# A spectral mixing and gated-convolution kernel: own buffers for the first stage of batch 0, a min form of the soft threshold, weight conversion in pairs of operations, operands at multiples of 128 bytes

## The chip, the core and the metric

The kernel runs on one core of a Trainium2 chip. The time is the device time of one execution in microseconds (us), the median of several; smaller is better. PE is the matrix engine (PEld its weight loads), DVE the vector engine, ACT the scalar engine, POOL the GpSimd engine, SP the engine whose queue issues all DMA transfers here. Each engine works through its own queue in order.

## What is computed

`x` is 8 x 3136 x 256. A real FFT along the sequence, a complex 256 x 256 mix with bias, a soft threshold, the inverse FFT; then a feed-forward layer with a convolution of three taps as its gate:

```python
X = np.fft.rfft(x, axis=1)
Yr = Xr @ w_r - Xi @ w_i + b_r
Yi = Xr @ w_i + Xi @ w_r + b_i
Yr = np.sign(Yr) * np.maximum(np.abs(Yr) - lam, 0.0)      # lam = 0.01, Yi likewise
x = np.fft.irfft(Yr + 1j * Yi, n=3136, axis=1)
h = np.maximum(x @ w_in, 0.0)                              # 256 -> 1024
conv_out = sum(conv_w[k] * shifted(h, k - 1) for k in range(3))
return h * sigmoid(conv_out) @ w_out                       # 1024 -> 256
```

`w_in`, `conv_w` and `w_out` arrive as float64 and are turned into two float32r parts, high and low, by integer operations on their bits.

## The kernel before

The length is split as 3136 = 56 x 56. The first half of the program is the spectral loop. For each batch, stage 1 (`stage1`, matmul L243) multiplies x by a 112 x 112 table, seven groups of four columns per batch; ACT copies each result from PSUM to `a1`, and a store writes `a1` to the DRAM scratch `sc1`. When all seven groups of a batch have landed, stage 2 reads them back transposed as `a2` (`load_a2`, L252). The loop goes over 56 items (8 batches x 7 groups). In iteration `it` stand: the load of `a2` for item it+2; stage 2 of item `it` (L262, 16 matmuls; ACT and DVE make `fh`, `fl`, `d` of it, L265 to L270); the mix of item it-1 (L286, 40 matmuls; ACT copies `p1`, DVE adds `v` in four parts, L294, then the threshold, L299 and L300; ACT rounds `v` to `sh`, L301, and POOL makes the rest `sl`, L302); stage 3 of item it-3 (L312, 12 matmuls, copied by ACT and stored to `sc2`); and stage 1 of later batches, some ten items ahead. Each matmul on float32 stands in the trace as two instructions, so an item's eight of L262 are 16 there and a stage 1 is four of L243.

The weights are loaded and converted inside this loop in eight pieces of 512 columns (`load_bits`, `from_bits`, `split_weight`, L194 to L211): every fifth iteration one piece is converted as a whole, by ten DVE operations and a copy on ACT. The convolution's weights (`load_conv`) follow in iteration 7.

The start differs: the seven groups of batch 0 go through the same buffers (three `xr`, two `a1`) with four PSUM buffers, the copies being shared by ACT and DVE (L245, L247). Tables and the weights of the mix are asked for after the last of these stores.

The second half, from about 600 us, is the feed-forward layer. Stage 4 (`stage4`, L389, seven per batch, each with one load of `z2` from `sc2`) ends the inverse transform: ACT writes `yh`, DVE `yl` (L395, L396). Then 28 chunks x 8 slices: `up` (L408, 12 matmuls of 450 columns), ReLU, the three taps, the sigmoid and the product on ACT and DVE, `gh` and `gl`; four slices later `down` (L436, 21 matmuls of 256 columns). The first batch's seven stage 4 have high priority.

A scheduler orders each engine's queue at compile time by a model of times, within the dependences; `tc.issue_after(ins)` puts what is traced in its block behind `ins` on that engine. Pools give out buffers (`bufs`) that are handed on when the last reader is done; with `reuse_waits="tile"` a new pool in old space waits for the tiles it overlaps alone. The lines on which the order around the change hangs:

```python
        DB, XRB, SL_ENG = 1, 3, nc.gpsimd
        AHEAD = NG + 3
        WP0, WPS = NG - 2, 5
```

## Time and profile before

| | |
|---|---|
| median of 3 runs | 1832.44 us (1827.99 to 1833.72) |
| profiled execution | 1831.85 us, its span 1830.0 us |
| busy in the span | PE 1778.5 (97%), PEld 1669.9 (91%), DVE 1557.2 (85%), ACT 1195.2 (65%), POOL 133.6 (7%) |
| DMA | 164.11 MB, mean 90 GB/s |
| granted TensorE clock | 0.989 of full speed |

Matmuls are pipelined: the profile lets each of them last until its results are out, so they overlap, and a busy PE is not a PE at its peak. A stage's rate is better read from the chain of waits, where consecutive pieces stand end to end, or from the count of instructions in a stretch. In rows of groups, after the bar, stand the busy time, the mean length of one in ns, and the idle time of the engine ahead of them with what ended it.

### The profile page before, as it was taken

The numbers are of one execution on the slowest core, as the hardware profiler recorded it, in microseconds if no ns is written. First come the engines' busy times: TensorE is split into PE (matmuls) and PEld (weight loads), VectorE is DVE, ScalarE is ACT, GpSimd is POOL, SyncE is SP. The second block draws the span as 40 slices with busy tenths as digits, with TensorE's granted clock in tenths as the row PEclk, the third lists the DMA queues.
The fourth block names the chain that finished last, engine by engine and source line by source line (L and its number), as shares of the span: only waits on it lengthen the run. The fifth ranks groups of instructions, "written<-read, shape, count | busy, mean of one in ns | idle before, by whom it ended". The sixth has DMA issues, their size and how long they took to land.

```text
span 1830.0 us, 29736 instructions
## 1 busy us (share of the span) xinstructions
PE 1778.5 (97%) x12320; PEld 1669.9 (91%) x12320; DVE 1557.2 (85%) x1788; ACT 1195.2 (65%) x1582; POOL 133.6 (7%) x60
## 2 busy tenths in 40 slices
PE   5889999999999899999999999999999999999998
PEld 3778789899899799999999999999999999999998
DVE  3899998888899598888888888888888888888887
ACT  2555556555555577777777667777767777776776
POOL 0122222222223100000000000000000000000000
PEclk8999999999999899999999999999999999999999
DMA  8676665665642311011111101111101111100001
GB/s 252 189 235 209 182 199 172 204 191 178 204 132 81 111 39 59 26 41 51 41 41 51 41 21 51 51 41 51 51 21 37 58 57 43 51 21 21 21 21 41
DMA packets 106682, 164.11 MB, mean 90 GB/s; under 512 B 8738, under 2 KB 85412, under 8 KB 106548
## 3 DMA queue, kind: packets, MB, share of 16 engines
q1 hardware_dynamic: 106548, 162.22, 29.4%
q8 instruction: 97, 1.59, 0.4%
q14 instruction: 37, 0.30, 0.1%
HBM read 85.13 MB, written 77.07 MB: 89 GB/s over the span
## 4 chain that ended last, share of the span: by engine, by line
PE 89%; DVE 6%; DMA 3%; issue 1%; ACT 0%; SPq 0%; ACTq 0%; DVEq 0%
PE acc L436 31%; PE ps_h L408 30%; PE ps_mx L286 12%; PE ps_s L389 5%; PE ps_s L262 4%; PE ps_s L243 3%; PE ps_s L312 3%; DVE v L294 1%; DVE fl L270 1%; DVE fl L268 1%; DMA a<-sc 1%; DMA sc<-a 1%; DVE v L300 1%; DMA z<-sc 1%; DMA t<-in_fwd_dram 0%
## 5 line engine op out<-in xcount | busy, mean ns | idle before, releaser
L436 PE MATMUL acc<-wout,gh 128*128 128x256 f32 x3136 | 578.3, 283 | 0.0
L417 DVE SCALAR_TENSOR_TENSOR c<-h,cw,c 128x896 f32<-128x896 f32 x448 | 513.0, 1147 | 52.7 <-ACT c L415 51.7
L408 PE MATMUL ps_h<-yh,win 128*128 128x450 f32 x1792 | 549.4, 367 | 1.3 <-ACT yh L395 1.2
L436 PEld LDWEIGHTS acc<-wout,gh 128*128 128x128 f32 x3136 | 497.0, 188 | 6.4
L436 PE MATMUL acc<-wout,gl 128*128 128x256 f32 x1568 | 441.0, 283 | 0.0
L410 ACT ACTIVATE h<-ps_h 128x900 f32<-128x900 f32 x224 | 207.6, 927 | 264.6 <-PE ps_h L408 264.4
L408 PEld LDWEIGHTS ps_h<-yh,win 128*128 128x128 f32 x1792 | 339.3, 189 | 27.3 <-ACT yh L395 1.5
L408 PE MATMUL ps_h<-yl,win 128*128 128x450 f32 x896 | 329.3, 368 | 0.4 <-DVE yl L396 0.4
L436 PEld LDWEIGHTS acc<-wout,gl 128*128 128x128 f32 x1568 | 294.1, 188 | 0.2
L423 DVE TENSOR_TENSOR gl<-c,gh 128x896 fp32r<-128x896 f32 x224 | 242.9, 1088 | 55.3 <-ACT gh L422 51.5
L419 DVE TENSOR_TENSOR c<-h,c 128x896 f32<-128x896 f32 x224 | 243.4, 1087 | 48.6 <-ACT c L418 48.1
L422 ACT CAST gh<-c 128x896 fp32r<-128x896 f32 x224 | 209.8, 942 | 49.2 <-DVE c L419 49.2
L418 ACT ACTIVATE c<-c 128x896 f32<-128x896 f32 x224 | 213.4, 953 | 26.1 <-DVE c L417 23.1
L286 PE MATMUL ps_mx<-wmix_lo,fh 128*128 128x256 f32 x672 | 202.4, 301 | 0.0
L286 PE MATMUL ps_mx<-wmix_hi,fl 128*128 128x256 f32 x672 | 193.4, 289 | 6.2 <-DVE fl L270 6.2
L286 PE MATMUL ps_mx<-wmix_hi,fh 128*128 128x256 f32 x672 | 197.5, 294 | 0.0
L408 PEld LDWEIGHTS ps_h<-yl,win 128*128 128x128 f32 x896 | 169.4, 189 | 10.3 <-DVE yl L396 0.9
L415 ACT ACTIVATE c<-h,cw 128x896 f32<-128x896 f32 x168 | 175.7, 1046 | 2.6 <-DVE gl L423 0.2
L302 POOL TENSOR_TENSOR sl<-v,sh 128x1024 fp32r<-128x1024 f32 x56 | 133.4, 2382 | 470.3 <-PE ps_s L312 289.0
L294 DVE TENSOR_TENSOR v<-ps_mx,p 64x512 f32<-64x512 f32 x224 | 153.9, 687 | 3.8 <-ACT p L288 0.3
L262 PEld LDWEIGHTS ps_s<-t,a 112*128 112x128 f32 x896 | 113.6, 199 | 42.5 <-DMA a<-sc 15.4
L286 PEld LDWEIGHTS ps_mx<-wmix_hi,fl 128*128 128x128 f32 x672 | 128.3, 191 | 16.6 <-issue 9.5
(90 smaller groups left out, 2145.8 us busy)
## 6 DMA issues: line engine op xcount, KB each, us to landing
xr<-in_x_dram SPq DMA_DIRECT2D x56, 448.0 KB, 4.5
sc<-a SPq DMA_DIRECT2D x56, 448.0 KB, 4.1
a<-sc SPq DMA_DIRECT2D x56, 448.0 KB, 4.8
sc<-z SPq DMA_DIRECT2D x56, 448.0 KB, 3.2
z<-sc SPq DMA_DIRECT2D x56, 448.0 KB, 3.8
out_dram<-o SPq DMA_DIRECT2D x27, 896.0 KB, 4.3
win_bits<-in_moe_w_in_dram SPq DMA_DIRECT2D x4, 512.0 KB, 4.9
wout_bits<-in_moe_w_out_dram SPq DMA_DIRECT2D x4, 512.0 KB, 5.2
```

Source lines behind the costliest of these rows:

```text
L262: nc.tensor.matmul(ps[:, k], a2[:, k, t * P:(t + 1) * P], t2[:, g * UG + k, :], start=(k == 0), stop=(k == UG - 1), skip_group_check=True)
L286: nc.tensor.matmul(ps[c][:, k, :], lt, rh, start=(n == 0), stop=(n == len(mm) - 1))
L294: nc.vector.tensor_tensor(v[dst, :, k, :], ps[c][src], p1[src], op=ALU.add)
L408: nc.tensor.matmul(ps[:, a, 0:CH + 2], lt, rh, start=(n == 0), stop=(n == len(mm) - 1))
L410: nc.scalar.activation(h, ps[:, :, 0:CH + 2], AF.Relu)
L415: nc.scalar.mul(c, h[:, :, 0:CH], cw[:, 0, f:f + 1])
L417: nc.vector.scalar_tensor_tensor(c, h[:, :, k:k + CH], cw[:, k, f:f + 1], c, op0=ALU.mult, op1=ALU.add)
L418: nc.scalar.activation(c, c, AF.Sigmoid)
L419: nc.vector.tensor_tensor(c, h[:, :, 1:CH + 1], c, op=ALU.mult)
L422: nc.scalar.copy(gh, c)
L423: nc.vector.tensor_tensor(gl, c, gh.bitcast(F32), op=ALU.subtract)
L436: nc.tensor.matmul(acc[m // 2][:, m % 2, :], lt[:, sl], rh[:, f, :], start=(f == 0 and n == 0 and m % 2 == 0), stop=(f == NF - 1 and n == ...
```

## The change

It has four parts.

- Head: the seven `x` loads of batch 0 go into seven buffers of their own (`hx`), the first one in two parts, and the results into seven buffers `ha`; the loads of tables, mix weights and bias stand between loads and stores. Two stages 1 of batch 1 are issued ahead of the first `a2` loads. The pools `wkf`, `wk`, `cab`, `io` are opened afterwards, in the space of these buffers.
- Threshold: instead of v - clip(v, -lam, lam) by two DVE operations, ACT makes r = relu(v - lam) and DVE one operation, min(v + lam, r).
- Weight conversion: `from_bits`, `split_weight` and `later` are generators now; from iteration 3 on two steps are taken per iteration, placed behind the threshold on DVE; from iteration 50 twelve. The convolution's weights come last.
- Places: `i2` and `cw` move behind the weights into one tile; rows of `y` get 3168 columns instead of 3138; small pads. In the program as built, all that PE reads in the second half, and `xr` and `f1`, starts at a multiple of 128 bytes. There are three `z2` buffers instead of two, and `h` has a pool of its own.

```diff
-    i2 = cst.tile([K1, K1], F32, name="i2")
-    cw = cst.tile([P, 3, NF], F32, name="cw")
+    cst.tile([P, 96], F32, name="pad")
     win = [cst.tile([P, NT, FF], F32R, name=f"win_{q}") for q in range(2)]
     wout = [cst.tile([P, NF, D], F32R, name=f"wout_{q}") for q in range(2)]
+    cst_s = cst.tile([P, 2 * P], F32, name="cst_s")
+    i2 = cst_s[0:K1, 0:K1]
...
-            v.tensor_scalar(e, hi, 20, 0x7FF, op0=ALU.logical_shift_right, op1=ALU.bitwise_and)
+            yield v.tensor_scalar(e, hi, 20, 0x7FF, op0=ALU.logical_shift_right, op1=ALU.bitwise_and)
...
+        def later():
+            pieces = []
...
+            for n in range(len(pieces) + 1):
+                if n < len(pieces):
+                    dst, src, nm = pieces[n]
+                    asked.append((dst, load_bits(src, WP, nm), WP, nm))
+                    yield None
+                if n:
+                    yield from split_weight(*asked.pop(0))
             nc.sync.dma_start(i2, inv2)
...
+        def stage1_head(xs, b=0):
+            with tc.tile_pool(name="ha", bufs=1, reuse_waits="tile") as ha:
+                for jc, xr in enumerate(xs):
+                    a1 = ha.tile([K1, JC, D], F32, name=f"ha{jc}")
...
-            cl = wk.tile([K2, UG, D], F32, name="cl", bufs=1)
-            nc.vector.tensor_scalar(cl, v, -LAM, LAM, op0=ALU.max, op1=ALU.min)
-            nc.vector.tensor_tensor(v, v, cl, op=ALU.subtract)
+            r = wk.tile([K2, UG, D], F32, name="r", bufs=1)
+            nc.scalar.activation(r, v, AF.Relu, bias=mlam)
+            thr = nc.vector.scalar_tensor_tensor(v, v, LAM, r, op0=ALU.add, op1=ALU.min)
...
-        WP0, WPS = NG - 2, 5
-        load_f1()
-        for p in range(NG):
-            ld = stage1(0, p, head=True)
-        with tc.issue_after(ld.ins):
-            load_t2(0)
-            load_mix()
-            load_bias()
+        WP0, LAST = 3, n_it - 6
+        load_f1()
+        with tc.tile_pool(name="hx", bufs=1, reuse_waits="tile") as hx:
+            xh = []
+            for p in range(NG):
+                xr, ld = load_x(hx, 0, p, parts=2 if p == 0 else 1, tag=f"hx{p}")
+                xh.append(xr)
+            with tc.issue_after(ld.ins):
+                load_t2(0)
+                load_mix()
+                load_bias()
+                st = stage1_head(xh)
+        with tc.issue_after(st.ins):
+            for _ in range(2):
+                stage1(*items[p1])
+                p1 += 1
+            for i in range(2):
+                a2s[i], ld = load_a2(*items[i])
...
-            while p1 < n_it and p1 < min(it + AHEAD, NG + 1 + it + it // 2):
+            while p1 < n_it and p1 < min(it + AHEAD, NG + 2 + it + it // 2):
...
-            if it == NG:
-                load_conv()
-            if it >= WP0 and it % WPS == 0 and later:
-                dst, src, nm = later.pop(0)
-                asked.append((dst, load_bits(src, WP, nm), WP, nm))
-            if it >= WP0 + WPS and it % WPS == 4 and asked:
-                split_weight(*asked.pop(0))
+            if WP0 <= it < n_it:
+                with tc.issue_after(ss[it - 1][2].ins):
+                    for _ in range(2 if it < LAST else 12):
+                        next(background, None)
...
-    zio, y_a = pool("zio", 2), pool("y_a")
-    wk, io, y_b = pool("cwk"), pool("cio"), pool("y_b")
+    zio, y_a = pool("zio", 3), pool("y_a")
+    wk, hp, io, y_b = pool("cwk"), pool("chp", 3), pool("cio"), pool("y_b")
+    SW = 3168
+    hp.tile([P, 8], F32, name="pad", bufs=1)
...
-        y = [(y_a, y_b)[b % 2].tile([P, NT, S + 2], F32R, name=nm) for nm in ("yh", "yl")]
+        y = [(y_a, y_b)[b % 2].tile([P, NT, SW], F32R, name=nm) for nm in ("yh", "yl")]
```

How the order of instructions moves is seen at three places. In the changed kernel line numbers differ: stage 1 of the head is L269 with copies L271 and L273, stage 1 L254, stage 2 L289, the mix L313, stage 3 L339, stage 4 L427, `up` L446, `down` L474.

SP's queue at the start, before: loads of `x` (L235) and stores of `a1` (L248) alternate from the fifth on, each load needing a free `xr`, each store its copies.

```order
L235 DMA xr_136<-in_x_dram 112x1024
L235 DMA xr_146<-in_x_dram 112x1024
L235 DMA xr_156<-in_x_dram 112x1024
L235 DMA xr_166<-in_x_dram 112x1024
L248 DMA sc1_0_57<-a1_138 112x1024
L235 DMA xr_176<-in_x_dram 112x1024
L248 DMA sc1_0_57<-a1_148 112x1024
L235 DMA xr_186<-in_x_dram 112x1024
L248 DMA sc1_0_57<-a1_158 112x1024
```

The same queue after, from the bias on; ahead of these rows stand the eight loads of `x` without a break, then t2 and the weights of the mix.

```order
L169 DMA b_raw_159<-in_b_i_dram 1x256
L274 DMA sc1_0_57<-ha0_167 112x1024
L274 DMA sc1_0_57<-ha1_175 112x1024
L274 DMA sc1_0_57<-ha2_183 112x1024
L274 DMA sc1_0_57<-ha3_191 112x1024
L274 DMA sc1_0_57<-ha4_199 112x1024
L274 DMA sc1_0_57<-ha5_207 112x1024
L274 DMA sc1_0_57<-ha6_215 112x1024
L245 DMA xr_225<-in_x_dram 112x1024
L245 DMA xr_235<-in_x_dram 112x1024
L279 DMA a2_245<-sc1_0_57 112x4x256
L279 DMA a2_247<-sc1_0_57 112x4x256
```

All loads of batch 0 now precede all stores, and two loads of batch 1 stand between the last store and the first `a2` load.

DVE's queue inside the loop where weights are converted, before: operations of a conversion (L194 to L211) stand between the four `v` of the mix (L294), between the two of the threshold (L299, L300), everywhere.

```order
L195 TENSOR_SCALAR win_e<-win_e 128x512
L270 TENSOR_TENSOR fl<-d,fh 128x2x256
L294 TENSOR_TENSOR v<-ps_mx_744,p_787 64x2x256 x2
L196 TENSOR_SCALAR win_e<-win_e 128x512
L294 TENSOR_TENSOR v<-ps_mx_745,p_787 64x2x256 x2
L197 SCALAR_TENSOR_TENSOR win_e<-win_bits,win_e 128x512
L299 TENSOR_SCALAR cl<-v 128x1024
L199 TENSOR_TENSOR win_m<-win_m,win_e 128x512
L202 SCALAR_TENSOR_TENSOR win_rest<-win_r,win_e 128x512
L300 TENSOR_TENSOR v<-v,cl 128x1024
```

DVE's queue after, one whole item from threshold (L327) to threshold.

```order
L327 SCALAR_TENSOR_TENSOR v<-v,r 128x1024
L194 TENSOR_SCALAR win_e<-win_e 128x512
L195 TENSOR_SCALAR win_e<-win_e 128x512
L294 TENSOR_TENSOR d<-ps_s_1413,d 128x256
L295 TENSOR_TENSOR fl<-ps_s_1413,fh 128x512
L294 TENSOR_TENSOR d<-ps_s_1422,d 128x256
L295 TENSOR_TENSOR fl<-ps_s_1422,fh 128x512
L321 TENSOR_TENSOR v<-ps_mx_1433,p_1476 64x2x256 x2
L297 TENSOR_TENSOR fl<-d,fh 128x2x256
L321 TENSOR_TENSOR v<-ps_mx_1434,p_1476 64x2x256 x2
L327 SCALAR_TENSOR_TENSOR v<-v,r 128x1024
```

Two operations of a conversion follow each threshold, and nothing stands between the last `v` and the threshold, which needs ACT's `r`.

SP's queue at the change to the second half, before: the first two loads of `z2` stand far ahead; the next ones follow the last stores of stage 3 (L315).

```order
L315 DMA sc2_7_72<-z1_6389 112x1024
L385 DMA z2_6491<-sc2_0_65 112x4x256
L385 DMA z2_6504<-sc2_0_65 112x4x256
L315 DMA sc2_7_72<-z1_6405 112x1024
L385 DMA z2_6517<-sc2_0_65 112x4x256
L385 DMA z2_6530<-sc2_0_65 112x4x256
L315 DMA sc2_7_72<-z1_6421 112x1024
```

The same place after.

```order
L423 DMA z2_6478<-sc2_0_65 112x4x256
L423 DMA z2_6491<-sc2_0_65 112x4x256
L423 DMA z2_6504<-sc2_0_65 112x4x256
L342 DMA sc2_7_72<-z1_6133 112x1024
L342 DMA sc2_7_72<-z1_6229 112x1024
L342 DMA sc2_7_72<-z1_6325 112x1024
L342 DMA sc2_7_72<-z1_6398 112x1024
L423 DMA z2_6517<-sc2_0_65 112x4x256
L423 DMA z2_6530<-sc2_0_65 112x4x256
L342 DMA sc2_7_72<-z1_6414 112x1024
```

Three loads now stand ahead of the last stores, and each later one stands one tile earlier against the stores.

More of the change, by code (lines that the diff above doesn't have):

```diff
@@ L237, in stage1 @@
             for j in range(0, JC, 2):
[L238 to L242 removed]
+                ps = ps1.tile([K1, 2, D], F32, name="ps_s1")
                 nc.tensor.matmul(ps, f1, xr[:, j:j + 2, :], start=True, stop=True)
[L244 to L247 removed]
+                nc.scalar.copy(a1[:, j:j + 2, :], ps)
@@ L248, in stage1 @@
             return nc.sync.dma_start(sc1[b][:, jc * JC:(jc + 1) * JC, :], a1)
+        def stage1_head(xs, b=0):
+            with tc.tile_pool(name="ha", bufs=1, reuse_waits="tile") as ha:
+                for jc, xr in enumerate(xs):
+                    a1 = ha.tile([K1, JC, D], F32, name=f"ha{jc}")
+                    for j in range(0, JC, 2):
+                        k = (jc * 2 + j // 2) % 4
+                        if k < 3:
+                            ps = psm.tile([K1, 2, D], F32, name="ps_s1h", tag=f"ps_mx{k}")
+                        else:
+                            ps = ps1.tile([K1, 2, D], F32, name="ps_s1")
+                        nc.tensor.matmul(ps, f1, xr[:, j:j + 2, :], start=True, stop=True)
+                        if j:
+                            nc.vector.tensor_copy(a1[:, j:j + 2, :], ps)
+                        else:
+                            nc.scalar.copy(a1[:, j:j + 2, :], ps)
+                    st = nc.sync.dma_start(sc1[b][:, jc * JC:(jc + 1) * JC, :], a1)
+            return st
@@ L315, in stage3 @@
             nc.sync.dma_start(sc2[b][:, g * UG:(g + 1) * UG, :], z1)
-        warm = stg.tile([P, 1], F32, name="warm")
+        nc.vector.memset(mlam, -LAM)
         nc.vector.memset(warm, 0.0)
```

94 lines of the change are left out of this document (45 added, 49 removed).

## The prediction

> **What bounds the kernel now.** I first read busy times by stage, cut where the page's TensorE row changes: the start, the early and the late spectral loop, its last items, the change to the second half, the second half. The columns are PE, PEld, DVE, ACT, POOL, clock, DMA share, GB/s.
>
> ```profile
> 0.00:42.00 42.00, 22.43 (x55) 11.35 (x56) 12.48 (x24) 10.64 (x19) 0.20 (x4) 0.81 0.83 249
> 42.00:254.00 212.00, 193.25 (x1343) 167.50 (x1341) 199.84 (x320) 115.68 (x204) 41.03 (x17) 0.97 0.69 202
> 254.00:519.00 265.00, 265.00 (x1966) 237.77 (x1964) 224.35 (x300) 155.04 (x274) 66.20 (x28) 1.00 0.63 187
> 519.00:596.00 77.00, 77.00 (x651) 76.50 (x650) 73.99 (x108) 43.70 (x74) 21.46 (x9) 1.00 0.36 106
> 596.00:639.00 43.00, 34.81 (x215) 32.09 (x215) 22.55 (x25) 21.31 (x22) 4.72 (x2) 0.88 0.41 118
> 639.00:1830.00 1191.00, 1185.96 (x8101) 1144.69 (x8100) 1024.01 (x1016) 848.80 (x991) 0.00 (x0) 1.00 0.13 40
> ```
>
> PE never stops from 254 to 596 nor, but for some 5 us at the end, from 639 on. Matmuls overlap, so what one costs comes from the chain, where nothing else stands between: item after item at 400 us, and the second half at 1016 us.
>
> ```profile
> 399.98 0.86 PE ps_s L243 x2
> 400.84 1.78 PE ps_s L262 x16
> 402.63 1.20 PE ps_mx L286 x10
> 403.83 0.86 PE ps_s L243 x2
> 404.69 3.60 PE ps_mx L286 x30
> 408.29 1.41 PE ps_s L312 x12
> ...
> 1015.96 1.68 PE ps_s L389 x15
> 1017.64 2.52 PE acc L436 x21
> 1020.16 2.46 PE ps_h L408 x12
> ```
>
> So 0.43 us for a matmul of L243, 0.111 for L262, 0.120 for L286, 0.1175 for L312, 0.112 for L389, 0.120 for L436, 0.205 for L408. An item of the spectral loop with its stage 1 takes 9.71 us, one without 7.99. The number of matmuls from 42 to 254 by line, L243, L262, L286, L312 in this order:
>
> ```profile
> 42.00:254.00 212.00, 43.99 (x83) 12.30 (x82) 0.97 0.69 202
> ...
> 42.00:254.00 212.00, 40.50 (x296) 38.51 (x295) 0.97 0.69 202
> ...
> 42.00:254.00 212.00, 113.25 (x760) 97.46 (x760) 0.97 0.69 202
> ...
> 42.00:254.00 212.00, 30.32 (x204) 25.96 (x204) 0.97 0.69 202
> ```
>
> At the prices above that is 35.7 + 32.9 + 91.2 + 24.0 = 183.8 us of work in 212: 28.2 us are lost there (18.75 of it idle, the rest half clock and pipeline refill behind the idle). In the same way 0 to 42 holds 30 matmuls of L243 and 26 of L262, 15.8 us, and loses 26.2; 596 to 639 holds 27 of L312, 128 of L389 and 60 of L408, 29.8 us, and loses 13.2. Nothing is lost between 254 and 596. All that the schedule can bring lies in these 67.6 us. Who held PE from 42 to 255, and at the change to the second half:
>
> ```profile
> PE ps_mx L286 <- DVE fl L270: 6.2, 4, 2.0
> PE ps_mx L286 <- DVE v L294: 4.9, 5, 1.6
> PE ps_s L262 <- DMA a<-sc: 3.5, 1, 3.5
> ...
> PE ps_s L389 <- DMA z<-sc: 6.5, 3, 3.5
> ```
>
> DVE is 94% busy from 42 to 254 (199.84 of 212), where the weights are converted.
>
> **The head.** The first item's first matmul is the row at 33.98; the chain of waits before it:
>
> ```profile
> 1.19 3.90 DMA xr<-in_x_dram
> 5.23 3.74 PE ps_s1h L243 x4
> 24.75 4.48 DMA sc<-a
> ...
> 29.31 0.34 SPq L252
> ...
> 30.23 7.09 DMA a<-sc
> ...
> 33.98 2.29 PE L262 MATMUL ps_s<-t,a 112*128 112x128 f32 x9 [10.89 <-DMA a<-sc]
> ...
> 12.00:15.00 3.00, 2.38 (x6) 0.62 (x4) 0.69 (x1) 0.59 (x1) 0.00 (x0) 1.00 0.99 336
> ```
>
> Before, a load waits for a buffer that a matmul frees, and stores wait behind such loads on SP's queue. Now seven loads go out at once, and the stores stand behind all of them and behind t2, the mix weights and the bias. What must have moved before the first a2 load is x (3.21 MB), the seven stores (3.21) and t2, f1 and the weights of the mix (0.8): 7.2 MB, at the 336 GB/s of the last row 21.5 us. The first 0.46 MB took until 5.1, so the stream began near 3.7 and ends at 25.2 if it never pauses. PE would be done earlier: from 4.4, four cold matmuls of 0.94 us (3.74/4) and 24 of 0.43 end at 18.5, copy and issue 1.0, a landing of 4.48 as in the row: 24.0. I take 24.5 for the last store. The pools that reuse the head's buffers write them after that and wait for nothing. Two x loads of batch 1 (0.92 MB, 2.7 us) are now queued ahead of the a2 loads; they move while SP waits for the last store, so a part of them hides. From SP's first issue of an a2 load, at 29.31, to the matmul it took 4.7 us. First item at 29.2 instead of 33.98; ends 26.5 and 32. Two halves of a new stage 1 (0.86) are done by then. The half clock that follows an idle PE stays: PE idles from 18.5 to 29 as it did from 24 to 34, and the rows of 0 to 42 and of 596 to 639 show 0.81 and 0.88 granted. Gain 5.6 with the moved stage 1, ends 3 and 8.
>
> **The threshold.** Removed on DVE, per item, are L299 and L300; added are one scalar_tensor_tensor there and one Relu on ACT:
>
> ```profile
> L299 DVE TENSOR_SCALAR cl<-v x56: 679/1576/2497, 58.6 to 597.3; 128x1024 f32<-128x1024 f32 x56
> ...
> L300 DVE TENSOR_TENSOR v<-v,cl 128x1024 f32<-128x1024 f32 x56 | 68.6, 1224 | 1.4
> L417 DVE SCALAR_TENSOR_TENSOR c<-h,cw,c 128x896 f32<-128x896 f32 x448 | 513.0, 1147 | 52.7 <-ACT c L415 51.7
> L301 ACT CAST sh<-v 128x1024 fp32r<-128x1024 f32 x56 | 58.8, 1050 | 82.1 <-DVE v L300 78.9 <-DVE cw L229 2.0 <-DVE cw_m L198 1.2
> L294 DVE TENSOR_TENSOR v<-ps_mx,p 64x512 f32<-64x512 f32 x224 | 153.9, 687 | 3.8 <-ACT p L288 0.3
> L210 DVE TENSOR_TENSOR win_m<-win_m,win 128x512 f32<-128x512 f32 x4 | 4.6, 1141 | 0.6 <-ACT win L209 0.6
> ```
>
> The new DVE operation is L417's kind on 1024 instead of 896: 1147 x 1024/896, at most 1.31, I take 1.28. DVE gives up 1.58 + 1.22 and takes 1.28: 1.5 us less per item. ACT takes 1.05 more; it was 155 of 265 us busy, so 5.7 of 9.71 becomes 6.8. In the late loop PE is the bound, and both are worth nothing there.
>
> The price is a new round trip: DVE waits for ACT between v (L294) and the threshold, and nothing of its queue stands between. Its loop per item is then four v 2.75, Relu 1.05, threshold 1.28, two conversions at most 2 x 0.69 (L210's undisturbed length, as L294's), d 2 x 0.42, fl 2 x 0.68, the last fl 0.69 (L267, L268 and L270 keep their shapes; 512 elements as in L294): 9.35. That is 0.36 below PE's 9.71. With 1.5 stages 1 per item, as early on, PE's item is longer still.
>
> **The weight conversion.** Ten DVE operations of each of eight pieces stood bunched in this stage, a piece every five items; now two operations follow each threshold from the fourth item on, at most 1.37 us per item, with the convolution's 27 small ones last. DVE's mean in the early loop falls from 94% to (8.2 - 1.5 + 1.4)/9.71 = 83%, 8.2 being the late loop's 224.35 over 27.3 items. The 11.1 us of waits for DVE in the list and the half clock behind them should go. What stays of 28.2: the wait for a2 at the change to batch 1 (3.5, and some 2.5 of half clock after it), since SP still holds that load until the last store of the batch has landed. I keep 6 and gain 22; ends 10 (all but the waits named DVE stay) and 27.
>
> From 519 to 596 no stage 1 is left and DVE was 96% busy against PE's 7.99 per item. There the round trip (10 items x 1.05) and the last 21 small operations, at
>
> ```profile
> L229 DVE TENSOR_TENSOR cw<-cw_m,cw_rest 128x8 f32<-128x8 f32 x3 | 0.5, 160 | 0.0
> ```
>
> 3.4 us, are set against 10 x 1.5 saved: near nothing. I take a loss of 1.5, ends 0 and 6.
>
> **The change to the second half.** Seven z loads feed its first tiles.
>
> ```profile
> 613.41 4.85 DMA z<-sc
> ...
> 620.76 1.12 ACT yh L395
> ...
> 621.90 1.13 DVE yl L396
> ```
>
> With two buffers the third to seventh were issued only when PE had read an earlier one, 4.85 us before they could be used; that is the 6.5 above. A third buffer moves each issue one tile earlier, some 2 to 3 us. But yh and yl, 2.25 us per tile, also hold the two PSUM buffers. Gain 3.5, ends 0 and 8.
>
> **Multiples of 128 bytes.** Before, i2 and cw (448 and 96 bytes) put win and wout 32 bytes past such a multiple, and a row of y of 12552 bytes puts its second half 8 further. After, all lie at a multiple. L286, whose operands lay so already, takes 0.120 for 256 columns; L436, off it, takes 0.120 as well: nothing to gain on 4704 matmuls. L408 has 450 columns. From the two, 0.44 ns per column; from L243 (two passes of 512 in 0.86, 0.42 each half) and L286's surplus 0.201 would be possible instead of 0.205: 2688 x 3.5 ns = 9.4 us at most, 0 at least. I take 3. The new places of h, z2, gh and gl change addresses alone, and PE covers what reads them.
>
> **Sum.** 5.6 + 22 - 1.5 + 3.5 + 3 = 32.6: span 1830.0 becomes 1797.4. The profiled execution took 1831.85 for its span, and the median of the runs, 1832.44, is 0.6 above it: 1800. With all ends at their best 1780, at their worst 1825.
>
> **Rivals.** (a) Slower: the round trip makes DVE the bound of the late loop. L299's median of 1576 against its shortest of 679 shows DVE held by POOL's subtraction (L302), and L210's mean of 1141 against 687 shows it for two SBUF operands. If the threshold and a conversion are each held 0.9, the loop is 11.15, 1.44 over PE's item; over 44 items that costs 63, and the time is 1863. It decides from 9.71 + 32.6/44 = 10.45 per item. Against it: Relu delays the threshold by just the time for which POOL held L299. Chance 4%.
>
> (b) Only the threshold is held, as L299 was, by 0.9: loop 10.25, 0.54 over, 44 items, 24 us: 1824. The Trainium skill says this, in SBUF — State Buffer, section SBUF: two separate sides: GpSimd and a DVE instruction with two SBUF inputs exclude each other for the whole instruction. By that rule the new operation, with v and r in SBUF, is no freer than the old one, and the sum is this 1824; without a meeting of the two it is 1800. The rows of L299 and L210 agree with the rule; whether the two meet depends on the time of Relu. Chance 10%.
>
> (c) The early loop is bound by DMA, not by DVE: the share of DMA is 0.83 in the first 42 us and i1, t2 and two weight pieces now queue up ahead of the fourth a2. Half of the 28.2 stays: 1808. For it: the share. Against: one wait of 3.5 named DMA. Chance 14%.
>
> (d) The alignment speeds all wide matmuls, L436 to L262's 0.111: 4704 x 9 ns and 9.4: 1752. Against it L286. Chance 5%.
>
> (e) Own buffers bring nothing in the head since DMA is the limit anyway: 1805, inside the forecast's range.
>
> **The numbers.** The forecast with (e) has 67%; a measurement of this kernel cannot tell less than 0.3%, 5.5 us, from no change. Faster by more: 0.67 + 0.14 + 0.05 and most of (b), 0.93 in all; within: 0.03; slower: 0.04. The range 1777 to 1821 takes in the forecast's ends but for the last 4 us, (c), and leaves out (a), (d) and most of (b).
>
> **What will show it.** The first matmul on a2 near 29; PE's idle time from 42 to 254 below 5 us, with DVE near 83%; the late item still 9.71; the seventh tile of the second half some 3 us earlier; L436 still 21 in 2.52, L408 12 in 2.42 to 2.46. I am wrong if waits for the threshold hold PE after 254, or if the matmuls of the second half change their pace by more than 2%.

## The result, and the profile after

The changed kernel takes 1806.47 us (median of 4 runs, 1805.84 to 1808.87) against 1833.08 for the kernel before on the same chip: a ratio of 0.9863, 95% interval 0.9842 to 0.9884. Its profiled execution has a span of 1807.1 us (before 1830.0) at a granted clock of 0.992.

The stretches answer to those of before, cut at the same events (columns as there):

```profile
0.00:42.00 42.00, 25.90 (x69) 12.31 (x70) 12.59 (x25) 11.48 (x22) 0.20 (x4) 0.80 0.93 263
42.00:254.00 212.00, 209.06 (x1529) 185.48 (x1529) 168.27 (x257) 146.53 (x249) 47.31 (x20) 1.00 0.70 214
254.00:519.00 265.00, 265.00 (x1993) 240.25 (x1993) 208.06 (x328) 182.85 (x306) 66.18 (x28) 1.00 0.62 188
519.00:574.00 55.00, 51.22 (x425) 50.10 (x423) 49.56 (x87) 33.27 (x51) 14.23 (x6) 1.00 0.33 98
574.00:615.00 41.00, 35.64 (x215) 33.18 (x214) 21.62 (x26) 23.04 (x25) 4.73 (x2) 0.88 0.42 124
615.00:1807.00 1192.00, 1187.56 (x8099) 1144.81 (x8098) 1023.79 (x1015) 848.04 (x990) 0.00 (x0) 1.00 0.13 40
```

The matmuls of 42 to 254 by line, L254, L289, L313, L339 in this order (PE, PEld, clock, DMA share, GB/s):

```profile
42.00:254.00 212.00, 47.09 (x92) 13.57 (x92) 1.00 0.70 214
...
42.00:254.00 212.00, 43.54 (x344) 41.96 (x344) 1.00 0.70 214
...
42.00:254.00 212.00, 123.86 (x865) 108.63 (x865) 1.00 0.70 214
...
42.00:254.00 212.00, 32.88 (x228) 28.48 (x228) 1.00 0.70 214
```

At the prediction's prices that is 39.6 + 38.2 + 103.8 + 26.8 = 208.3 us of work in 212: 3.7 lost, before 28.2. Counted in the same way, 0 to 42 holds 32 matmuls of stage 1, 25 of L289 and 12 of L313 (18.0 us; 24.0 lost, before 26.2); 519 to 574 holds 425 at 7.99/68 us (49.9; 5.1 lost, before none in the last items); 574 to 615 holds 24 of L339, 128 of L427, 60 of L446 and 3 of L474 (29.8; 11.2 lost, before 13.2). The second half takes 1192 for 8099 matmuls, before 1191 for 8101. So the 22.9 us between the two spans are +2.2 at the head, +24.5 in the early loop, -5.1 in the last items, +2.0 at the change to the second half and -1 behind it; that adds up to 22.6, and 0.3 is what counting at the cuts leaves.

The late item and the pace of the second half have not moved. From the chain of waits (the columns are start, length, what):

```profile
402.50 1.78 PE ps_s L289 x16
...
412.20 1.78 PE ps_s L289 x16
```

```profile
1016.18 2.46 PE ps_h L446 x12
1018.64 2.51 PE acc L474 x21
```

One item is 9.70 us, and 12 and 21 matmuls take what they took before to 0.01 us. The threshold (L327) in the late loop, shortest, median and longest in ns, and one of its operations with the POOL operation that it meets:

```profile
L327 DVE SCALAR_TENSOR_TENSOR v<-v,r x28: 1224/1369/1381, 258.3 to 516.8; 128x1024 f32<-128x1024 f32 x28
...
403.77 1.37 DVE L327 SCALAR_TENSOR_TENSOR v<-v,r 128x1024 f32<-128x1024 f32 x1 [2.11 <-ACT r L326]
...
401.70 2.36 POOL L329 TENSOR_TENSOR sl<-v,sh 128x1024 fp32r<-128x1024 f32 x1 [7.33 <-PE ps_s L339]
```

The head, however, came out otherwise than forecast. Its chain of waits, and with it two rows of the engines' own timelines (behind the bar of a timeline row, in brackets, stands the idle time ahead of it and what ended it):

```profile
19.41 0.64 DVE wm L158
...
24.69 4.81 DMA sc<-ha
...
29.65 5.09 DMA a<-sc
...
34.88 3.75 PE ps_s L289 x16
```

```profile
19.41 0.69 DVE L158 TENSOR_TENSOR wm<-wm_raw,wm_raw 128x512 f32<-128x512 f32 x1 [4.42 <-DMA wm_raw<-in_w_i_dram]
```

```profile
31.35 2.05 PE L254 MATMUL ps_s<-xr,f 112*112 112x512 f32 x2 [6.09 <-DMA xr<-in_x_dram]
```

The last store was issued at 24.69, where before it was issued at 24.75; the first stage 2 stands at 34.88, 0.9 later than before. DVE waited 4.42 us for the second half of the mix weights, with the copies of stage 1 queued behind, and PE 6.09 us for the first x of batch 1.

The 2.2 us that the head gained all the same did not come with the first item. The granted clock was 0.50 from 33 to 37 us in both kernels; in the changed one, where PE had stage 1 of batch 1 from 31.35 on, the full clock was back earlier. Before and after, from 40 to 45 us (PE, PEld, DVE, ACT, POOL, clock, DMA share, GB/s):

```profile
40.00:45.00 5.00, 5.00 (x27) 3.94 (x27) 2.08 (x5) 2.31 (x5) 0.00 (x0) 0.69 1.04 273
```

```profile
40.00:45.00 5.00, 4.97 (x37) 4.31 (x36) 3.88 (x8) 4.29 (x10) 0.00 (x0) 1.00 1.03 277
```

That the stage 1 brought the clock back is not shown by a run of its own.

### The profile page after: what moved, and what is told of

Its sections match the earlier page's. It is cut to its first block, busy times and chain, and to the rows that moved or that the text cites. A ratio compares the mean times of both kernels' runs of the same rounds, so it can differ in the third digit from the quotient of the medians.

```text
span 1807.1 us, 29723 instructions
## 1 busy us (share of the span) xinstructions
PE 1774.4 (98%) x12320; PEld 1666.1 (92%) x12320; DVE 1483.9 (82%) x1733; ACT 1245.2 (69%) x1638; POOL 132.7 (7%) x60
## 4 chain that ended last, share of the span: by engine, by line
PE 93%; DVE 3%; DMA 2%; ACT 1%; issue 1%; SPq 0%; ACTq 0%; DVEq 0%
PE acc L474 31%; PE ps_h L446 30%; PE ps_mx L313 13%; PE ps_s L427 5%; PE ps_s L289 5%; PE ps_s L254 4%; PE ps_s L339 4%; DVE v L321 1%; DMA wm_raw<-in_w_i_dram 1%; DVE fl L297 1%; DMA a<-sc 1%; ACT r L326 0%; DMA xr<-in_x_dram 0%; DVE fl L295 0%; DMA sc<-ha 0%
## 5 line engine op out<-in xcount | busy, mean ns | idle before, releaser
L474 PE MATMUL acc<-wout,gh 128*128 128x256 f32 x3136 | 577.2, 283 | 0.0
L455 DVE SCALAR_TENSOR_TENSOR c<-h,cst_s,c 128x896 f32<-128x896 f32 x448 | 513.2, 1147 | 53.2 <-ACT c L453 52.2
L446 PE MATMUL ps_h<-yh,win 128*128 128x450 f32 x1792 | 552.0, 368 | 1.4 <-ACT yh L433 1.2
L474 PEld LDWEIGHTS acc<-wout,gh 128*128 128x128 f32 x3136 | 501.0, 191 | 6.8
L474 PE MATMUL acc<-wout,gl 128*128 128x256 f32 x1568 | 441.9, 283 | 0.0
L446 PEld LDWEIGHTS ps_h<-yh,win 128*128 128x128 f32 x1792 | 340.1, 190 | 27.0 <-ACT yh L433 1.4
L446 PE MATMUL ps_h<-yl,win 128*128 128x450 f32 x896 | 329.7, 368 | 0.7 <-DVE yl L434 0.7
L474 PEld LDWEIGHTS acc<-wout,gl 128*128 128x128 f32 x1568 | 298.7, 191 | 0.2
L313 PE MATMUL ps_mx<-wmix_hi,fh 128*128 128x256 f32 x672 | 211.0, 314 | 0.0
L313 PE MATMUL ps_mx<-wmix_hi,fl 128*128 128x256 f32 x672 | 191.4, 286 | 3.9 <-DVE fl L297 3.8
L313 PE MATMUL ps_mx<-wmix_lo,fh 128*128 128x256 f32 x672 | 191.0, 284 | 0.0
L446 PEld LDWEIGHTS ps_h<-yl,win 128*128 128x128 f32 x896 | 170.0, 190 | 11.6 <-DVE yl L434 1.0
L453 ACT ACTIVATE c<-h,cst_s 128x896 f32<-128x896 f32 x168 | 175.5, 1045 | 2.5
L329 POOL TENSOR_TENSOR sl<-v,sh 128x1024 fp32r<-128x1024 f32 x56 | 132.5, 2365 | 449.2 <-PE ps_s L339 384.9
L327 DVE SCALAR_TENSOR_TENSOR v<-v,r 128x1024 f32<-128x1024 f32 x56 | 78.7, 1404 | 83.6 <-ACT r L326 83.4
L313 PEld LDWEIGHTS ps_mx<-wmix_hi,fh 128*128 128x128 f32 x672 | 128.4, 191 | 12.3 <-issue 12.0
```

The costliest lines, as they stand in the source:

```text
L313: nc.tensor.matmul(ps[c][:, k, :], lt, rh, start=(n == 0), stop=(n == len(mm) - 1))
L329: SL_ENG.tensor_tensor(sl, v, sh.bitcast(F32), op=ALU.subtract)
L446: nc.tensor.matmul(ps[:, a, 0:CH + 2], lt, rh, start=(n == 0), stop=(n == len(mm) - 1))
L453: nc.scalar.mul(c, h[:, :, 0:CH], cw[:, 0, f:f + 1])
L455: nc.vector.scalar_tensor_tensor(c, h[:, :, k:k + CH], cw[:, k, f:f + 1], c, op0=ALU.mult, op1=ALU.add)
L474: nc.tensor.matmul(acc[m // 2][:, m % 2, :], lt[:, sl], rh[:, f, :], start=(f == 0 and n == 0 and m % 2 == 0), stop=(f == NF - 1 and n == ...
```

## Experiments

The kernel before ran beside each group of experiments (1835.26, 1832.36 and 1832.32 us), so the kernels are compared by their ratios to it. The changed kernel has 0.9863. "Lost" is meant as in the prediction: time less the priced matmuls, here from the trace's whole list of matmul starts, which puts the changed kernel at 3.6 in the early loop (45 to 254 us).

**The early loop: conversion and threshold, each taken back.** Conversion bunched (c1):

```diff
-            if WP0 <= it < n_it:
-                with tc.issue_after(ss[it - 1][2].ins):
-                    for _ in range(2 if it < LAST else 12):
-                        next(background, None)
+            if it % 5 == 4:
+                for _ in range(11):
+                    next(background, None)
```

> The changed kernel, but the weight conversion is bunched again: eleven steps in every fifth iteration, anywhere on DVE, instead of two behind each threshold. Theory A: the spreading brought the gain of the early loop; then the stretch 42 to 254 loses 18 to 24 us more than the changed kernel's 4, with waits of PE for fl and v, and the time is 1820 to 1830. Rival: the shorter threshold and the earlier stage 1 of batch 1 brought it; then the time stays within 6 us of 1806.5.

1815.79 us, ratio 0.9896 (0.9881 to 0.9911): Theory A's direction, but less than it expected; the early loop lost 15.8 us more, and the last items, where the changed kernel loses 5.1, lost nothing. The edit takes back two things at once, the pairs and their place behind the threshold; no run parts them. The old threshold (t1):

```diff
-            nc.scalar.activation(r, v, AF.Relu, bias=mlam)
-            thr = nc.vector.scalar_tensor_tensor(v, v, LAM, r, op0=ALU.add, op1=ALU.min)
+            nc.vector.tensor_scalar(r, v, -LAM, LAM, op0=ALU.max, op1=ALU.min)
+            thr = nc.vector.tensor_tensor(v, v, r, op=ALU.subtract)
```

> The changed kernel with the old threshold, clip and subtraction both on DVE; all else stays. Theory A: the min form brought little in the early loop, and the round trip through ACT costs 5 to 6 us in the last items (time 540 to 575, where fl at L297 takes 2.08 instead of 0.69 us because POOL's subtraction now falls on it). Then the early loop loses 2 to 5 us more, the last items lose nothing but the 2 us of the small operations, and the time is 1801 to 1807. Rival: half of the gain of the early loop is the 1.5 us per item that the min form takes off DVE; then the early loop loses 10 or more again and the time is 1812 to 1820.

1805.88 us, ratio 0.9841 (0.9827 to 0.9856), an interval that overlaps the changed kernel's: in Theory A's range, with only 0.8 us more lost in the early loop where it had expected 2 to 5. In the last items it lost 4.2 us where the small operations stand (twice the 2 expected) and nothing behind them; L297 stayed at 0.69. Both taken back:

> The changed kernel with both taken back: the bunched conversion (as in the run with it alone) and the old threshold on DVE. Head, places and z2 buffers stay. The early loop (45 to 254) lost 28.2 us before, 3.6 in the changed kernel, 4.4 with the old threshold alone, 19.4 with the bunched conversion alone. Theory A: DVE's load while a piece is converted is what PE waits for, so the two savings add where it is bunched: 26 to 29 lost here, time 1818 to 1824. Rival: stage 1 of batch 1, which the new head does earlier, brought the 9 us between 28.2 and 19.4: then 19 to 21 lost here, and the time is that of the bunched conversion alone, ratio to before 0.990.

1819.37 us, ratio 0.9929 (0.9914 to 0.9943). The same stretch of the three kernels, bunched, old threshold, both:

```profile
42.00:254.00 212.00, 200.37 (x1411) 174.03 (x1411) 190.41 (x313) 138.55 (x233) 45.58 (x19) 0.98 0.71 214
```

```profile
42.00:254.00 212.00, 208.75 (x1523) 184.91 (x1522) 194.22 (x274) 126.33 (x227) 47.31 (x20) 1.00 0.70 214
```

```profile
42.00:254.00 212.00, 198.06 (x1403) 171.94 (x1403) 202.77 (x330) 119.19 (x212) 44.59 (x18) 0.99 0.70 213
```

Against 1529 matmuls of the changed kernel and 1343 of before, the old threshold alone gives 1523, the bunched conversion 1411, both 1403. The early loop loses 4.4, 19.4 and 20.9 us. So the spreading brings 15.8 to 16.5 us there. The min form's 0.8 to 1.5 is less than two executions of one order of instructions differ by in this loop (2.6 us, l0 below), so no worth of it is shown. What it spreads is not DVE's total: with the old threshold DVE is busy 194.22 of 212, more than with the bunched conversion (190.41), and PE hardly waits. The third run decides between the 26 to 29 of its Theory A and the 19 to 21 of its rival: the rival holds for the loop, and 7.2 of the 28.1 us lost before come from neither edit. (Its time is in Theory A's range all the same, 3.6 us above the bunched conversion alone: 1.5 in this loop, 1.3 at the head, the rest behind.) In the kernel with both taken back no wait for an `a2` load stands among PE's, which was 3.5 us before; that fits the stage 1 that it does earlier, but the bunched kernel, which does it earlier too, still shows one of 1.6 us, no run took it alone away, and what makes up the 7.2 stays open.

**The last items.** Three conversion steps per iteration from the 20th on, none behind the 47th (c2):

```diff
-                    for _ in range(2 if it < LAST else 12):
+                    for _ in range(2 if it < 20 else 3):
```

> The changed kernel, but from iteration 20 on three conversion steps per iteration instead of two, so that all are done by iteration 47 and no twelve at once stand in iterations 50 and 51. Theory A: those small operations make DVE late in the last items, and from then on POOL's subtraction falls on fl (L297, 2.08 us instead of 0.69) in each of them, so that DVE and not PE sets the pace (9.2 instead of 7.99 us per item). Then here L297 stays at 0.69 to the end, the stretch 540 to 575 loses under 1 us instead of 5 to 6, and the time is 1800 to 1803 where the changed kernel has 1806.5. Rival: three steps per iteration make DVE the bound of the late loop already; then 254 to 519 takes up to 8 us more and the time is 1808 to 1814.

1800.3 us, ratio 0.9822 (0.9807 to 0.9838). The timelines of DVE (L197, one of the small operations, and L297) and of POOL (L329) in the last items, changed kernel first:

```profile
531.51 1.55 DVE L197 TENSOR_SCALAR cw_m<-cw_bits 128x8 int32<-128x8 int32 x1
...
538.72 2.85 DVE L297 TENSOR_TENSOR fl<-d,fh 128x512 fp32r<-128x512 f32 x1
...
548.12 2.57 DVE L297 TENSOR_TENSOR fl<-d,fh 128x512 fp32r<-128x512 f32 x1
```

```profile
530.66 2.38 POOL L329 TENSOR_TENSOR sl<-v,sh 128x1024 fp32r<-128x1024 f32 x1 [5.61 <-PE ps_s L339]
538.64 2.38 POOL L329 TENSOR_TENSOR sl<-v,sh 128x1024 fp32r<-128x1024 f32 x1 [5.61 <-PE ps_s L339]
547.78 2.36 POOL L329 TENSOR_TENSOR sl<-v,sh 128x1024 fp32r<-128x1024 f32 x1 [6.75 <-PE ps_s L339]
```

and the same with three steps per iteration:

```profile
536.74 0.69 DVE L297 TENSOR_TENSOR fl<-d,fh 128x512 fp32r<-128x512 f32 x1
```

```profile
537.83 2.39 POOL L329 TENSOR_TENSOR sl<-v,sh 128x1024 fp32r<-128x1024 f32 x1 [5.61 <-PE ps_s L339]
545.82 2.38 POOL L329 TENSOR_TENSOR sl<-v,sh 128x1024 fp32r<-128x1024 f32 x1 [5.60 <-PE ps_s L339]
```

POOL starts when stage 3 has given its one `sl` buffer back, at a time that PE sets. With three steps `fl` has ended 0.4 us before that, and items follow each other 7.99 us apart, PE's own pace. In the changed kernel the bunch of small operations has made DVE late, and one of them met POOL itself: L197, 0.17 us elsewhere in the bunch, took 1.55 and ended with POOL's operation of 530.66. In the old threshold's run L195 took 2.19 in the same way, beside a POOL operation that starts at 540.04, and PE's one wait in its last items, 2.5 us for `fl`, follows that. From then on `fl` in the changed kernel starts 0.1 to 0.9 us behind POOL's start and ends 0.6 us after POOL does, in each of four items, and this keeps DVE late: 9.1 to 9.3 us from one POOL operation to the next. From 520 to 570 us PE lost nothing with three steps and 5.0 us in the changed kernel.

The same items without POOL's subtraction (l0):

```diff
-        def mix(xs):
+        def mix(xs, low):
...
-            sl = wk.tile([K2, UG, D], F32R, name="sl", bufs=1)
+            sl = wk.tile([K2, UG, D], F32R, name="sl", bufs=1) if low else sh
...
-            SL_ENG.tensor_tensor(sl, v, sh.bitcast(F32), op=ALU.subtract)
+            if low:
+                SL_ENG.tensor_tensor(sl, v, sh.bitcast(F32), op=ALU.subtract)
...
-                ss[it - 1] = mix(xs.pop(it - 1))
+                ss[it - 1] = mix(xs.pop(it - 1), it - 1 < 45)
```

> The changed kernel, but in the items from the 45th on POOL's subtraction (L329) is left out, and stage 3 reads sh in place of sl there: the low part of v is missing in them. The twelve small operations stay in iterations 50 and 51. Theory A (POOL holds fl): L297 is 0.69 throughout, and the last items lose at most 2 to 3 us, at the small operations alone. Rival (the round trip through ACT alone, 1.2 us of waiting for r in each item, sets the pace): the last items go on at 9 us or more and lose 5 us as before.

1799.18 us, ratio 0.9818 (0.9799 to 0.9837); `fl` takes 0.69 throughout and nothing is lost up to 570, with the small operations and the round trip both in place. The two together cost nothing once POOL is silent, so it is POOL that holds `fl`.

The old threshold with three steps (the edits of t1 and c2 together, tc):

> The changed kernel with the old threshold on DVE and three conversion steps per iteration from the 20th on (no twelve at once). With two steps and the old threshold DVE was busy 248.09 of 265 us in the late loop, 9.09 per item; a third step of 0.69 makes it 9.78 against PE's 9.71. Theory A: the min form is worth what it takes off a full DVE and nothing else; here the late loop loses 2 to 8 us and the time is 1802 to 1808, above the 1800.3 of the same steps with the min form. Rival: the min form's saving is not needed even here, since the steps of the convolution's weights take 0.16 each and DVE has items in hand: 254 to 519 loses nothing, L297 stays at 0.69 in the last items, and the time is 1798 to 1801.

1803.18 us, 1797.53 to 1806.3, ratio 0.9835 (0.9811 to 0.9858). The late loop lost nothing (Theory A is wrong there, although the time lies in its range), and the interval overlaps that of c2: no worth of the min form can be told from these two.

**The head.** Tables behind the stores (h1):

```diff
             with tc.issue_after(ld.ins):
-                load_t2(0)
-                load_mix()
-                load_bias()
                 st = stage1_head(xh)
         with tc.issue_after(st.ins):
+            load_t2(0)
+            load_mix()
+            load_bias()
             for _ in range(2):
                 stage1(*items[p1])
```

> The changed kernel, but t2, the mix weights and the bias are asked for behind the seven stores of the head instead of ahead of them; the own buffers stay. Theory A: the first item came at 34.88 and not at 29.2 because DVE's queue held the mix weights' subtraction (L158), which waited 4.42 us until 19.41 for its load, ahead of three copies of stage 1. Then the last store is issued near 19.5 instead of 24.69, the first stage 2 stands at 29.0 to 30.5, and the time is 4 to 5.5 us below the changed kernel's 1806.5: about 1801.5. Theory B: the head is bound by the bytes that the DMA queues must move, in whatever order; then the first stage 2 stays at 33.5 or later and the time within 1.5 us of 1806.5.

1804.9 us, ratio 0.9838 (0.9822 to 0.9855). From its chain of waits:

```profile
21.88 0.30 SPq L274
...
27.41 7.36 DMA a<-sc
...
34.78 3.75 PE ps_s L289 x16
```

DVE's copies are free and the last store is issued 2.8 us earlier, but `a2` now takes 7.36 us to land instead of 5.09, and the first item stands where it stood. Theory A falls; as to the first item Theory B holds. The lower time does not come from the head: at 45 us the two kernels have lost 24.05 and 24.24. It comes from the early loop (2.2 us) and from behind 520 us (4.6). The first is no more than executions of one order of instructions differ by (l0, the same as the changed kernel up to the 45th item, lost 1.0 in the early loop where that lost 3.6). The second is the clock at the change to the second half: PE is busy for the same 32.6 of 38 us in the changed kernel, in u1 (below) and in h1, but at three granted clocks (0.87, 0.96, 1.00):

```profile
572.00:610.00 38.00, 32.64 (x207) 30.50 (x206) 18.58 (x23) 19.22 (x20) 4.73 (x2) 0.87 0.46 134
```

```profile
572.00:610.00 38.00, 32.63 (x215) 30.27 (x215) 21.60 (x27) 23.09 (x24) 4.73 (x2) 0.96 0.49 134
```

```profile
572.00:610.00 38.00, 32.58 (x229) 30.36 (x228) 23.12 (x27) 24.67 (x27) 4.73 (x2) 1.00 0.45 134
```

From 570 us to the first `down` the three lose 11.7, 8.5 and 6.9 us. Since u1 has the changed kernel's order of instructions, an order does not settle such a difference; why the clock falls behind nearly the same pauses in one execution and not in another, no run here shows.

In h2 the two `a2` loads also stand ahead of the two stages 1 of batch 1:

> As the run before (tables behind the stores), and the first two a2 loads also stand ahead of the two x loads of batch 1. If those x loads delay the a2 loads (Theory C: share of the queues), the first stage 2 comes 1 to 2.5 us earlier than in the run before, and the time is 1 to 2 us less, about 1800; if they only fill the time in which SP waits for the last store (Theory A alone), the first stage 2 comes at most 0.7 us earlier and batch 1's stage 1 is later: the same time within 1 us, or up to 2 more.

1804.57 us, ratio 0.9835 (0.9816 to 0.9854).

```profile
22.67 4.88 DMA sc<-ha
...
27.63 3.64 DMA a<-sc
...
31.41 3.75 PE ps_s L289 x16
```

The first item comes 3.4 us earlier than in h1, more than Theory C had allowed for: `a2` lands in 3.64 us when no x loads are ahead of it. Of this 1.8 us are left at 45 us, and 0.5 at 254.

In b2 the conversion steps of c2 are added to h2; in b4 t2 goes back ahead of the stores, and the mix weights and the bias stand behind `a2` (against b2):

```diff
             with tc.issue_after(ld.ins):
+                load_t2(0)
                 st = stage1_head(xh)
         with tc.issue_after(st.ins):
-            load_t2(0)
-            load_mix()
-            load_bias()
             for i in range(2):
                 a2s[i], ld = load_a2(*items[i])
         with tc.issue_after(ld.ins):
+            load_mix()
+            load_bias()
             for _ in range(2):
                 stage1(*items[p1])
```

> The changed kernel with three of the findings put together: tables behind the stores, the first two a2 loads ahead of the x loads of batch 1, and three conversion steps per iteration from the 20th on. If the gains add (some 1.5 us at the head, 5.5 in the last items): ratio to before 0.981 to 0.983, 1798 to 1801. If the head's gain is taken back in the loop, the ratio stays at the 0.982 of the conversion steps alone.

> As the run before, but the mix weights and the bias are asked for behind the first two a2 loads; ahead of them stand only x, t2 and the stores. Theory B (the head is bound by bytes): 0.53 MB less ahead of a2 at some 270 GB/s make the first stage 2 1.5 to 2.5 us earlier than the 31.4 of the kernel with a2 ahead of batch 1's x: 29 to 30. Theory L (it is bound by the latency of copy, store and load: last store issued near 22.7, 4.9 us to land, 3.6 for a2): it stays at 30.8 to 31.5. In both the mix starts later, since its weights land later, so that the time is within 1.5 us of the run before.

b2: 1802.94 us, ratio 0.9837 (0.9821 to 0.9852), above both of its expectations. b4: 1798.29 us (1797.9 to 1798.55), ratio 0.9815 (0.98 to 0.9829). The chain of b4, and its first stage 2 in PE's timeline:

```profile
21.73 3.81 DMA sc<-ha
```

```profile
29.43 3.71 PE L289 MATMUL ps_s<-t,a 112*128 112x128 f32 x16 [8.50 <-DMA a<-sc]
```

The first item stands at 29.43, 1.7 us ahead of b2's 31.15 and 2.0 ahead of h2's. That is Theory B's 0.53 MB (2.0 us at the 263 GB/s of the changed kernel's first 42 us); 1.1 of the 2.0 shows in the shorter landing of the last store (3.81 instead of 4.88), 0.9 in its earlier issue. b4 is the fastest of all, below the changed kernel with intervals that do not touch. b2 is not, 4.7 us behind b4 where at most 1.5 were expected: it lost 5.7 us in the early loop, where b4 lost 3.6 and c2 2.9, with the same steps there. Why is open.

**Places and buffers.** In u1 `win`, `wout`, `y`, `gh` and `gl` go back off the multiples of 128 bytes; every engine's order is the same:

```diff
-    cst.tile([P, 96], F32, name="pad")
+    cst.tile([P, 104], F32, name="pad")
...
-    cst_s = cst.tile([P, 2 * P], F32, name="cst_s")
+    cst_s = cst.tile([P, 2 * P + 24], F32, name="cst_s")
...
-    SW = 3168
-    hp.tile([P, 8], F32, name="pad", bufs=1)
+    SW = 3170
+    hp.tile([P, 16], F32, name="pad", bufs=1)
```

> The changed kernel with the places of before in the second half: win and wout 32 bytes past a multiple of 128, the y rows 8 bytes longer, gh and gl at 64; all engines' orders are the same, only addresses differ. Theory A: places cost nothing; L446's 12 in 2.46 and L474's 21 in 2.51 to 2.52 stay, and the time is the changed kernel's within 1.5 us, ratio to before 0.986. Rival: the multiples of 128 bytes brought the 3 us of the prediction, or up to 9.4: then L446's 12 take 2.46 here and 2.42 to 2.45 in the changed kernel, and this one is 3 to 9 us slower.

1807.56 us, ratio 0.986 (0.9843 to 0.9878). What PE did from 639 to 1795 us, where it never stopped, in the kernel before, the changed one and this one:

```profile
639.00:1795.00 1156.00, 1156.00 (x7886) 1115.67 (x7886) 999.71 (x993) 827.85 (x965) 0.00 (x0) 1.00 0.13 40
```

```profile
639.00:1795.00 1156.00, 1156.00 (x7870) 1114.24 (x7869) 996.05 (x989) 825.39 (x965) 0.00 (x0) 1.00 0.13 40
```

```profile
639.00:1795.00 1156.00, 1156.00 (x7855) 1111.49 (x7854) 993.93 (x986) 825.05 (x963) 0.00 (x0) 1.00 0.13 39
```

The window falls on another part of the second half in each kernel, so its counts (7886 before, 7870, 7855 in u1) show the direction better than the size. From the first `down` (L474, before L436) to the end of the span the work is the same, and it took 1191.0 us before, 1192.4 in the changed kernel and 1195.0 in u1; in nine of the other runs, which leave these alignments as they are, 1192.4 to within 0.02. So going off the multiples cost 2.6 us here, which taken alone would pass for the 3 of the prediction. But the kernel before, off the multiples too, was 1.4 us faster than the changed one. Addresses move the pace by some 0.2%; that multiples of 128 are the rule is not borne out, and what made the kernel before faster is open, since more than addresses differs there. This run also shows how far two executions of one order of instructions differ: from 520 us to the first `down` it lost 13.7 us, the changed kernel 16.6.

Two `z2` buffers instead of three (z2):

```diff
-    zio, y_a = pool("zio", 3), pool("y_a")
+    zio, y_a = pool("zio", 2), pool("y_a")
```

> The changed kernel with two buffers for z2 instead of three. Theory A: the third buffer brought some 2.5 to 4 us at the change to the second half; then a wait of the fourth to seventh tile for z2's load comes back (6.5 us of them before) and the time is 1809 to 1810.5. Rival: ACT's yh and DVE's yl with the two PSUM buffers set the pace of these tiles anyway; then the time is within 1 us of 1806.5.

1810.34 us, ratio 0.9877 (0.9858 to 0.9895). From its list of waits at the change:

```profile
PE ps_s L427 <- DMA z<-sc: 2.9, 2, 2.3
PEld ps_s L427 <- DVE yl L434: 2.5, 1, 2.5
PE ps_s L427 <- DVE yl L434: 2.3, 1, 2.3
```

The wait for a `z2` load is back, 2.9 us, where the changed kernel has none, and the time is in Theory A's range. Its mechanism is shown; the size is smaller in the traces: up to 570 us this execution and the changed kernel's have lost the same, from there to the first `down` they lose 13.2 and 11.7, so the third buffer brought 1.5 us between these two, less than the 2.5 to 4 that Theory A had named. (The medians of this run and u1, which share the runs of the kernel before, are 2.8 us apart, but u1 pays 2.6 for its addresses and was spared 3 by the clock.)

## Why the prediction was right, and where not

The time, 1806.47, lies inside the range (1777 to 1821) and on the side forecast, 6.5 above the 1800 named. By the terms of the sum:

| term | predicted (ends) | measured |
|---|---|---|
| head, 0 to 42 | +5.6 (3, 8) | +2.2 |
| early loop, 42 to 254 | +22 (10, 27) | +24.5 |
| last items | -1.5 (0, -6) | -5.1 |
| change to the second half | +3.5 (0, 8) | +2.0 |
| multiples of 128 (all of the second half) | +3 (0, 9.4) | -1 |
| sum | 32.6 | 22.6 (the spans: 22.9) |

- **The head: wrong.** The step that failed is "7.2 MB, at the 336 GB/s of the last row 21.5 us". The last store, taken as landed at 24.5 (below the 25.2 at which the same paragraph lets the stream end), landed at 29.50; `a2` then took 5.4 us to the first matmul, where 4.7 were taken. The row of 336 was one of 3 us; over 0 to 42 us the changed kernel moved 263 GB/s at a DMA share of 0.93, and before it was 249 at 0.83. With the two x loads of batch 1 and the first `a2`, 7.2 + 0.9 + 0.5 = 8.6 MB stand ahead of the first item: 25.6 us at 336, 32.7 at 263, and it came at 34.88. The second failed step is that the two x loads "move while SP waits for the last store": taking them away brought 3.4 us (h2 against h1). A third fault, DVE's wait for the mix weights ahead of the copies, was overlooked and did not matter, since h1 took it away for nothing. Rival (e), DMA as the limit of the head, fits the first item, which came no earlier than before; the forecast's range took it in. The 2.2 us gained are below the lower end of 3 and came by another way, the earlier return of the full clock, of which the prediction had said that it stays as it was: that much is luck.
- **The early loop: right in size, right in its main cause.** The waits named DVE have gone by the spreading (16 of the 24.5, shown by c1, t1 and ct; 7.2 come from neither the spreading nor the threshold, and their cause is open). But DVE's share, 79% (168.27 of 212, forecast 83%), was not the cause: at 92% (t1) PE lost hardly more. And 2.3 of the 6 us that were kept as lost went as well. PE's idle time there is 2.9 us (212 less 209.06), forecast below 5.
- **The threshold: right.** The late item stayed at 9.70. The median of L327 in the late loop is 1.37 against 1.22 undisturbed: held by 0.15 and not by rival (b)'s 0.9, since Relu delays it until POOL has 0.3 us left, as the prediction had argued against rival (a). The min form was not needed for it: with the old threshold (t1) PE lost no more in the late loop. The rule that the prediction weighed, the exclusive lock in the Trainium skill, SBUF — State Buffer, section SBUF: two separate sides, agrees with this trace all the same: where two operations met for longer it struck `fl` (L297, two SBUF inputs, 2.85 and 2.57 us in the rows above against 0.69 without POOL).
- **The last items: mechanism missed, size inside the ends.** The step put the round trip and the small operations, 0.16 us each, against 10 x 1.5 saved; together they cost nothing without POOL (l0). That the size fell inside the ends is luck. What cost 5.1 us is POOL holding one small operation and then `fl`, into which the small operations pushed DVE, and from which nothing brought it back.
- **The change to the second half: right** in mechanism (z2) and within what executions differ by, which is 3 us here.
- **Multiples of 128: wrong.** The step that failed is "from the two, 0.44 ns per column", which made two lines of different shape into a rate that another address could reach. The lower end, 0, was the row's own answer (L286 against L436). What u1 and the kernel before show in its place is a pace that moves by 2.6 and 1.4 us in opposite directions off the multiples.

The head and the alignment together make 7.4 of the 10.0 us between the sums of 32.6 and 22.6; the last items make 3.6 more and the change to the second half 1.5, and 2.5 came back in the early loop.

## What to carry to other kernels

Where one engine feeds another through a few buffers, look at the longest run of foreign operations in its queue, not at its share: conversion steps in bunches of eleven stopped PE with DVE 90% busy, the same steps in pairs, each behind a threshold, did not at 92%. Small operations are not cheap by their length alone: where another engine's operation can hold them, one of 0.17 us took 1.55. A head that only moves data is bounded by the bytes ahead of the first item at the rate of the whole stretch, and a load that is put ahead of it costs its bytes. Background work that ends in a bunch can leave an engine late for good where another engine's operation then holds it in each round: spread it so that it ends before the slack does.

## What the hardware showed

- An operation of 0.69 us with two SBUF inputs took 2.0 to 2.9 when it started just behind a POOL subtraction of 2.36 us, and the meeting repeated itself in each of four items; without the POOL operation it took 0.69 in each. One with a single input and 8 elements (L197) took 1.55 instead of 0.17 beside the same subtraction.
- With nothing but addresses changed, the same matmuls took 1195.0 instead of 1192.4 us (0.2%), where nine runs with the changed kernel's alignments agree with it to 0.02 us; being off the multiples of 128 was once the slower and once, in the kernel before (1191.0), the faster.
- With PE busy for 32.6 of the same 38 us, the granted clock was 0.87, 0.96 and 1.00 in three executions, which lost 11.7, 8.5 and 6.9 us around there; the first two have the same order of instructions.
- 263 GB/s was what loads and stores, most of 448 KB, reached together over the first 42 us with the DMA engines' share at 0.93; the 336 that the prediction took stood in a row of 3 us.
